# Attention matmuls in one float32r pass from pair 22 on, weights' sums moved to other stages, right pools at multiples of 64 bytes

## The chip, the cores and the metric

One core of one Trainium2 chip. The metric is device time in microseconds (us) of one execution; the runs shown are the median of three. Everything below is float32 in and out; float32r is the type in which TensorE takes a float32 word in one pass.

## The reference

Chunked attention, then two feed-forward layers, over 4608 tokens of 512 features:

```
for each batch (8), head (8), chunk of 64 tokens (9 of them), d = 64:
    s = q k^T / 8 ; p = exp(s - max) / (sum + 1e-9) ; o = p v
x  = o as [4608, 512]
h  = x @ w_in [512, 2048] ; g = h if h > 0 else exp(min(h, 0)) - 1 ; y = g @ w_out [2048, 512]
out = (sigmoid(y @ w_gate) * (y @ w_val)) @ w_out2      # w_gate, w_val [512, 1536], w_out2 [1536, 512]
```

Weights arrive as float64 and are converted on the chip.

## The kernel before

**Precision.** A product of two float32 matrices is made of three passes over float32r halves (`PASSES`, line 33): each operand is split in a high and a low part (`split`, line 94), and high-high, low-high and high-low are added in PSUM. The attention alone uses plain float32 matmuls, which TensorE carries out in several passes of its own: each stands twice in the records.

**Phase A** runs nine blocks of 512 tokens, each with 16 slots (`slot(s)`, line 358; s = 16 * block + f). A slot makes 12 matmuls `h` (`layer_1`, line 322: 128x512 columns) and 12 matmuls `y` for the slot two before (`layer_2`, line 330). Between them the two other engines make the activation: ScalarE (ACT) takes exp and relu (lines 302 and 305) and the high half (line 90), VectorE (DVE) the sum (line 308) and the low half (line 96).

**Attention is woven into the slots**, a pair of chunk groups (128x256 scores) in two slots, for the block after the current one. Even slot: `scores` (line 234, four matmuls of 64 columns; operands in `raw`, zero-padded on the host so that two chunks share one array), `softmax_max`, `softmax_exp`, `softmax_sum` (lines 248 to 264). Odd slot: `transposes` on TensorE (line 266), copied out by ACT (line 276), and in the next odd slot `values` (line 278) and `values_out`. 64 pairs go this way; 8 more open the program in `first_block`.

**Conversion of weights.** `convert` makes the first layer's weights in block 0. `convert_pairs` (line 566) makes the sums that the gate, value and output weights need (seven products of blocks in place of eight), 18 pairs of weight tiles. Each is a list of small steps in `todo`; `bg(n)` (line 102) takes n of them at four places of a slot. They spread over blocks 1 to 7, about three steps a slot, and their results go to DRAM (`wd`).

**Phase B.** Gate and value (`unit`, line 757): 36 units of 7 products, each product 12 matmuls of 384 columns; `xc`, the split input, is the moving operand and the weight tile the stationary one (line 772). Weight tiles are loaded ahead by `hold` (line 700), up to `RING` = 26 of 32 buffers. The output layer (`product`, line 897): 9 groups of 7 products, each 36 matmuls of 256 columns; here `gc`, the split gated input, is stationary (line 909).

**Where those operands lie.** `xc`, `gc`, `sg`, `vt` come from `get` (line 675), which takes the first name of `idle`: six buffers of pool `six_r`, on the right side of the memory, and seven of `six_l`, on the left. In the built program every `six_r` buffer begins 32 bytes past a multiple of 64, every `six_l` buffer and every weight tile at a multiple of 64. Followed through `idle`, the `xc` tiles of the six thirds of gate and value lie on the right in 6, 3, 4, 4, 3 and 4 of 7 cases (24 of 42; each tile serves six units), and 27 of 63 products' worth of `gc` tiles do.

Of the kernel before, what the change touches and what calls it, by code (L numbers as in the profile page):

```python
# [36 lines left out]
NP = NG // 2 - PB  # L37

# [4 lines left out]
FIRST_STEPS, A0_STEPS, A8_STEPS = 3, 9, 2  # L43
# [8 lines left out]
def kernel(  # L52
# [3 lines left out]
    qkv_1: bass.AP,  # L56
    w_in: bass.AP,
# [28 lines left out]
    ps_a = ctx.enter_context(tc.tile_pool(name="ps_a", bufs=2, space=bass.MemoryType.PSUM))  # L86
# [115 lines left out]
    def phase_a():  # L202
        with (
# [5 lines left out]
            e4 = c_p.tile([128, 4, CH + 1], F32, name="e4")  # L209

            raws, vals, st = {}, {}, {}

            def bank(n):
                return ps_a.tile([128, 512], F32, tag="a", name="bank")[:, 0:n]

            def load_raw(P):
                if P < NP:
                    raws[P] = a_p.tile([128, 2, 384], F32, tag="raw", name="raw")  # L220
                    nc.sync.dma_start(out=raws[P], in_=qkv_1[P][:, :, 0:384])

            def load_values(P):
                if 0 <= P < NP:
# [8 lines left out]

            def scores(P):
                ps, r = bank(256), raws.pop(P)
                st[P, "s"] = ps
                for i in range(2):
                    for a in range(2):
                        nc.tensor.matmul(  # L239
                            out=ps[:, (2 * i + a) * CH:(2 * i + a + 1) * CH],  # L240
                            lhsT=r[:, i, a * 128:(a + 1) * 128],
                            rhs=r[:, i, 256 + a * CH:256 + (a + 1) * CH],
# [3 lines left out]
                load_raw(P + 1)  # L246

            def softmax_max(P):
                s = st[P, "sc"] = a_p.tile([128, 4, CH], F32, tag="s", name="s")
                m = a_p.tile([128, 4, 1], F32, tag="m", name="m")  # L250
                ps = st.pop((P, "s"))
                ps = ps.rearrange("p (n k) -> p n k", n=4)
                nc.vector.tensor_reduce(out=m[:, :, 0], in_=ps, op=ALU.max, axis=AX.X)
                nc.vector.tensor_tensor(out=s, in0=ps, in1=m.to_broadcast([128, 4, CH]), op=ALU.subtract)
# [4 lines left out]
            def softmax_sum(P):  # L259
                d = a_p.tile([128, 4, 1], F32, tag="d", name="d")  # L260
# [16 lines left out]

            def values(P):
                t = st.pop((P, "t"))
                ps, r = bank(256), vals.pop(P)  # L280
                st[P, "v"] = ps
                for i in range(2):
                    for u in range(2):
                        nc.tensor.matmul(  # L284
                            out=ps[:, 128 * i + u * CH:128 * i + (u + 1) * CH],
                            lhsT=r[:, i, u * 128:(u + 1) * 128],
                            rhs=t[:, 128 * i + u * CH:128 * i + (u + 1) * CH],
# [70 lines left out]
            def slot(s, steps=0):  # L358
# [8 lines left out]
                def is_pair(n):  # L367
                    return 0 <= n < NP

# [721 lines left out]
```

## Time and profile before

| | |
|---|---|
| median of 3 runs | 1769.94 us (1769.7 to 1770.62) |
| the profiled execution | 1771.81 us, span 1770.0 us |
| PE (matmul) busy | 1750.8 us, 99% of the span |
| DVE, ACT busy | 1085.0 us (61%), 717.7 us (41%) |
| DMA | 289.5 MB, mean 164 GB/s |
| block 0 with what opens it | until about 140 us |
| blocks 1 to 8 | about 140 to 958 us |
| gate and value | 958 to 1496 us |
| output layer | 1496 to 1765 us |

How to read it: a matmul's record is longer than the array's work for it, since matmuls overlap; so TensorE's pace is read from one start to the next. Idle time of an engine is listed with what ended it.

### The profile page before, as it was taken

How to read it: one execution, taken by the hardware profiler on the slowest of the kernel's cores; microseconds unless marked ns; L12 is line 12 of the kernel's file. 1: busy time of each engine (PE TensorE's matmuls, PEld its weight loads, DVE VectorE, ACT ScalarE, POOL GpSimd, SP SyncE). 2: the span in 40 equal slices, each digit the busy share in tenths (PEclk: the TensorE clock that was granted, in tenths of full speed). 3: DMA queues.
4: the chain of work that ended last, by engine and by line, in shares of the span. 5: the costliest groups of instructions: out<-in, count | busy, mean ns of one | idle time of the engine just before them, and what ended most of it. 6: DMA issues, size and time to landing. Idle time of an engine off the chain costs nothing.

```text
span 1770.0 us, 25620 instructions
## 1 busy us (share of the span) xinstructions
PE 1750.8 (99%) x10012; PEld 1600.3 (90%) x10012; DVE 1085.0 (61%) x1811; ACT 717.7 (41%) x1254; POOL 143.6 (8%) x264
## 2 busy tenths in 40 slices
PE   7999999999999999999999999999999999999998
PEld 6888888888888888888888999999999999999998
DVE  7997565655645455465342565656565656777775
ACT  7775454544545454454443121212121212433433
POOL 1000000000100000000021111111111120000000
PEclk9899999999999999999999999999999999999999
DMA  6654454544534324343278748483848397645451
GB/s 231 199 183 128 146 155 134 155 153 128 178 116 143 114 89 131 116 143 104 68 235 228 231 118 275 119 274 118 275 117 275 119 327 217 177 138 150 136 150 48
DMA packets 183431, 289.50 MB, mean 164 GB/s; under 512 B 10000, under 2 KB 125712, under 8 KB 183312
## 3 DMA queue, kind: packets, MB, share of 16 engines
q1 hardware_dynamic: 137232, 147.87, 27.2%
q0 software_dynamic: 46080, 140.00, 25.8%
q8 instruction: 79, 1.29, 0.3%
q14 instruction: 40, 0.33, 0.1%
HBM read 207.62 MB, written 80.22 MB: 163 GB/s over the span
## 4 chain that ended last, share of the span: by engine, by line
PE 97%; ACT 1%; DMA 1%; DVE 0%; SPq 0%; issue 0%; ACTq 0%
PE h L189 23%; PE y L338 22%; PE bx L772 9%; PE by L772 8%; PE bz L772 8%; PE by L909 4%; PE bx L909 4%; PE bz L909 4%; PE bw L772 4%; PE bank L239 3%; PE bank L284 3%; PE bw L909 2%; PE bank L270 1%; DMA qkv<-in_qkv 0%; DMA ymid<-y 0%; ACT xr L521 0%
## 5 line engine op out<-in xcount | busy, mean ns | idle before, releaser
L189 PE MATMUL h<-xs,w 128*128 128x512 f32 x1728 | 435.4, 400 | 1.3 <-DVE xs L531 1.3
L338 PE MATMUL y<-g,w 128*128 128x512 f32 x1728 | 422.3, 393 | 0.0
L338 PEld LDWEIGHTS y<-g,w 128*128 128x128 f32 x1728 | 320.4, 188 | 66.0
L189 PEld LDWEIGHTS h<-xs,w 128*128 128x128 f32 x1728 | 317.3, 190 | 63.8 <-DVE xs L531 1.7
L308 DVE SCALAR_TENSOR_TENSOR elu<-h,elu 128x512 f32<-128x512 f32 x144 | 99.4, 690 | 172.3 <-ACT elu L305 172.1
L772 PE MATMUL bx<-xc,w 128*128 128x384 f32 x864 | 164.9, 339 | 1.9 <-ACT sg L794 1.9
L772 PE MATMUL by<-xc,w 128*128 128x384 f32 x864 | 163.8, 338 | 0.0
L772 PE MATMUL bz<-xc,w 128*128 128x384 f32 x864 | 163.5, 337 | 0.0
L302 ACT ACTIVATE elu<-h 128x512 f32<-128x512 f32 x144 | 85.8, 596 | 179.0 <-PE h L189 178.3
L772 PEld LDWEIGHTS bx<-xc,w 128*128 128x128 f32 x864 | 153.7, 189 | 2.3 <-ACT sg L794 2.2
L772 PEld LDWEIGHTS by<-xc,w 128*128 128x128 f32 x864 | 153.0, 188 | 0.0
L772 PEld LDWEIGHTS bz<-xc,w 128*128 128x128 f32 x864 | 152.7, 188 | 0.0
L96 DVE TENSOR_TENSOR g<-elu,g 128x512 fp32r<-128x512 f32 x128 | 88.1, 688 | 76.9 <-ACT g L90 76.6
L90 ACT CAST g<-elu 128x512 fp32r<-128x512 f32 x144 | 89.3, 620 | 83.5 <-PE y L338 55.3
L715 POOL DMA_DIRECT2D w<-wd_glu x147 | 77.7, 529 | 510.1 <-DVE xc L96 215.5
L807 ACT ACTIVATE sg<-bx 128x384 f32<-128x384 f32 x36 | 17.7, 491 | 221.6 <-PE bx L772 221.5
L815 ACT ACTIVATE sg<-sg 128x1152 f32<-128x1152 f32 x36 | 42.0, 1168 | 151.0 <-DVE sg L791 151.0
L305 ACT ACTIVATE elu<-elu 128x512 f32<-128x512 f32 x144 | 91.2, 633 | 1.9
L96 DVE TENSOR_TENSOR gc<-c,gc 128x768 fp32r<-128x768 f32 x72 | 65.6, 953 | 28.7 <-ACT gc L90 28.7
L772 PE MATMUL bw<-xc,w 128*128 128x384 f32 x432 | 81.6, 337 | 0.0
L909 PE MATMUL by<-w,gc 128*128 128x256 f32 x648 | 80.1, 282 | 0.0
L909 PE MATMUL bx<-w,gc 128*128 128x256 f32 x648 | 79.8, 281 | 0.0
(116 smaller groups left out, 2229.6 us busy)
## 6 DMA issues: line engine op xcount, KB each, us to landing
w<-wd_glu POOLq DMA_DIRECT2D x147, 512.0 KB, 5.1
gv<-sg SPq DMA_DIRECT2D x36, 768.0 KB, 6.1
c<-gv SPq DMA_DIRECT2D x72, 384.0 KB, 5.2
raw<-in_qkv SPq DMA_DIRECT2D x64, 384.0 KB, 3.5
vals<-in_qkv SPq DMA_DIRECT2D x64, 256.0 KB, 3.4
wd_glu<-h POOLq DMA_DIRECT2D x12, 1024.0 KB, 6.5
w<-wd_out POOLq DMA_DIRECT2D x21, 512.0 KB, 5.1
wd_glu<-h POOLq DMA_DIRECT2D x12, 768.0 KB, 4.2
```

The costliest lines, as they stand in the source:

```text
L90: nc.scalar.copy(out=out, in_=raw)
L96: lo_eng.tensor_sub(out=lo, in0=raw, in1=hi)
L189: nc.tensor.matmul(out=ps, lhsT=w[:, zw, kk * 128:(kk + 1) * 128], rhs=xs[key, kk][:, zx], start=(kk == 0 and n == 0), stop=(kk == KC - 1 ...
L239: nc.tensor.matmul(out=ps[:, (2 * i + a) * CH:(2 * i + a + 1) * CH], lhsT=r[:, i, a * 128:(a + 1) * 128], rhs=r[:, i, 256 + a * CH:256 + ( ...
L284: nc.tensor.matmul(out=ps[:, 128 * i + u * CH:128 * i + (u + 1) * CH], lhsT=r[:, i, u * 128:(u + 1) * 128], rhs=t[:, 128 * i + u * CH:128 ...
L302: nc.scalar.activation(out=e_t[s], in_=h_t[s], func=ACTF.Exp)
L305: nc.scalar.activation(out=e_t[s], in_=e_t[s], func=ACTF.Relu, scale=-1.0, bias=1.0)
L308: nc.vector.scalar_tensor_tensor(out=e_t[s], in0=h_t.pop(s), scalar=0.0, in1=e_t[s], op0=ALU.max, op1=ALU.subtract,)
L338: nc.tensor.matmul(out=y_t[j, e], lhsT=w[:, zw, e * 128:(e + 1) * 128], rhs=g[:, zx], start=(f == 0 and n == 0), stop=(f == F1 - 1 and n = ...
L715: nc.gpsimd.dma_start(out=t, in_=wd[m][q][:, (LEFT if m == "glu" else RIGHT)[i]])
L772: nc.tensor.matmul(out=ps[m, c], lhsT=w[:, b, zw, 128 * k:128 * k + 128], rhs=xc[j, i][:, zx, k], start=(i < 4 and k == 0 and p == 0), sto ...
L909: nc.tensor.matmul(out=po[c][:, m], lhsT=t[:, zx, q % 3, 128 * m:128 * m + 128], rhs=w[:, q % 2, zw], start=(i < 4 and q == 0 and p == 0 a ...
```

## The change

**Attention from pair 22 on** (`P32`; slots from `TURN` = 40, block 2, to the end of block 7: 42 pairs). Loads bring the values once, unpadded (`raw2`). `split_k` and `split_qkv` make float32r halves on the chip; q's high half stands in one half of the partitions and its low half in the other, so that one matmul of 256 columns against k's high and low parts gives a product of two halves: four matmuls of 256 columns for the scores, four for the values. The two column groups are added outside TensorE (`first_parts` on ACT, an add on DVE). The transposes on TensorE are gone: `blocks_out` transposes 32x32 blocks on DVE and moves them over partitions by eight DMAs of 16 KB on SP's queue; `transposes_split` makes the halves two slots later. The scores and the values share one pair of PSUM banks. TensorE, a pair's two slots, before (`bank`: attention's PSUM; `h`, `y`: the layer's):

```order
L284 MATMUL bank<-t,vals 128x64 x4
L189 MATMUL h<-xs_4115,w 128x512 x3
L189 MATMUL h<-xs_4118,w 128x512 x3
L189 MATMUL h<-xs_4121,w 128x512 x3
L189 MATMUL h<-xs_4124,w 128x512 x3
L270 MATMUL bank<-ident,p 128x128 x2
L338 MATMUL y_4315<-g,w 128x512 x3
L338 MATMUL y_4316<-g,w 128x512 x3
L338 MATMUL y_4317<-g,w 128x512 x3
L338 MATMUL y_4318<-g,w 128x512 x3
L239 MATMUL bank<-raw 128x64 x4
```

and now:

```order
L284 MATMUL banks<-kz,qv 128x256 x4
L194 MATMUL h<-xs_7378,w 128x512 x3
L194 MATMUL h<-xs_7381,w 128x512 x3
L194 MATMUL h<-xs_7384,w 128x512 x3
L194 MATMUL h<-xs_7387,w 128x512 x3
L445 MATMUL y_7596<-g,w 128x512 x3
L445 MATMUL y_7597<-g,w 128x512 x3
L445 MATMUL y_7598<-g,w 128x512 x3
L445 MATMUL y_7599<-g,w 128x512 x3
L383 MATMUL banks<-pt,qv 128x256 x4
```

The transposes' row has gone, and both attention rows have four matmuls of 256 columns in place of 64. DVE in two slots past slot 40, before:

```order
L253 TENSOR_REDUCE m<-bank 128x4
L254 TENSOR_TENSOR s<-bank,m 128x256
L601 TENSOR_SCALAR t<-t 128x512
L604 SCALAR_TENSOR_TENSOR t<-wraw,t 128x512
L96 TENSOR_TENSOR g<-elu,g 128x512
L261 TENSOR_REDUCE d<-e_111 128x4
L262 RECIPROCAL d<-d 128x4
L264 TENSOR_TENSOR p<-e_111,d 128x256
L308 SCALAR_TENSOR_TENSOR elu<-h,elu 128x512
L610 ISA t<-wraw,t 128x1024
L648 TENSOR_TENSOR h_6105<-s,h_6105 128x4x256
L96 TENSOR_TENSOR g<-elu,g 128x512
```

Now the even slot and the beginning of the odd one (`kz`, `qv`: halves of k, and of q and v; `pt`: halves of the transposed weights; `tt`, `dt`: the transposed blocks after and before the DMAs):

```order
L314 TENSOR_TENSOR s<-banks,s_5095 64x256 x2
L315 TENSOR_REDUCE m<-s 128x4
L316 TENSOR_TENSOR s<-s,m 128x256
L97 CAST pt<-tt 64x512
L101 TENSOR_TENSOR pt<-tt,pt 64x512
L323 TENSOR_REDUCE d<-e_112 128x4
L324 RECIPROCAL d<-d 128x4
L326 TENSOR_TENSOR p<-e_112,d 128x256
L343 STREAM_TRANSPOSE dt<-p 128x4x2x32
L101 TENSOR_TENSOR g<-elu,g 128x512
L415 SCALAR_TENSOR_TENSOR elu<-h,elu 128x512
L252 CAST kz<-raw 128x2x256
```

and the rest of the odd slot, up to the sum of the next slot:

```order
L252 CAST kz<-raw 128x2x256
L399 TENSOR_TENSOR xr_5049<-banks,s_5162 64x256 x2
L260 TENSOR_TENSOR kz<-raw,kz 128x2x256
L261 TENSOR_TENSOR qv<-raw,qv 64x2x256
L262 TENSOR_TENSOR qv<-raw,qv 64x2x256
L101 TENSOR_TENSOR g<-elu,g 128x512
L415 SCALAR_TENSOR_TENSOR elu<-h,elu 128x512
```

The weight conversion's rows (`t`, `h_6105`) have gone from these slots, and 13 instructions of the attention stand where 5 stood; the two last `qv` rows are what the next slot's scores wait for, the `pt` rows what the next slot's values wait for.

**Weights' sums.** Pairs 0 to 8 (`PAIRS_A`) are made in slots 16 to 39, six steps a slot; pairs 9 to 17 from slot 4 of block 8 on, four steps a slot from slot 5 on, and then one step after each product of gate and value, in buffers of the weight pool. Until all are made, `hold` keeps 19 tiles, not 26. DVE in a unit of gate and value, before:

```order
L829 TENSOR_TENSOR sg<-vt,sg 128x1152
L791 TENSOR_TENSOR sg<-bw,sg 128x384
L791 TENSOR_TENSOR vt<-bw,vt 128x384
L791 TENSOR_TENSOR sg<-by,sg 128x384
L791 TENSOR_TENSOR vt<-by,vt 128x384
L791 TENSOR_TENSOR sg<-bz,sg 128x384
L791 TENSOR_TENSOR vt<-bz,vt 128x384
```

and now (`ct`, `cs`, `ch`: a weight pair, its sums, their halves):

```order
L987 TENSOR_TENSOR sg<-vt,sg 128x1152
L745 SCALAR_TENSOR_TENSOR ct<-craw,ct 128x512
L948 TENSOR_TENSOR sg<-bw,sg 128x384
L948 TENSOR_TENSOR vt<-bw,vt 128x384
L751 ISA ct<-craw,ct 128x1024
L948 TENSOR_TENSOR sg<-by,sg 128x384
L948 TENSOR_TENSOR vt<-by,vt 128x384
L764 TENSOR_TENSOR cs<-ct 128x256
L765 TENSOR_TENSOR cs<-ct 128x256
L948 TENSOR_TENSOR sg<-bz,sg 128x384
```

Each product's two adds are followed by one step of the conversion.

**Right pools.** A pool of 32 bytes is opened first on the right side, and small tiles grow to multiples of 64 bytes. In the built program every `six_r` buffer now begins at a multiple of 64, and so do the new attention tiles.

```diff
+TURN = 40
+P32 = TURN // 2 + 2
+PAIRS_A = 9
...
+    pad_p = ctx.enter_context(tc.tile_pool(name="pad", bufs=1, side="right"))
+    pad_p.tile([128, 8], F32, name="pad")
...
+            def split_k(P):
+                k = kz[P] = s_p[0].tile([128, 2, 2, 256], F32R, tag="kz", name="kz")
+                nc.vector.tensor_copy(out=k[:, :, 0], in_=raws[P][:, :, 256:512])
+            def split_qkv(P):
...
+                nc.scalar.copy(out=t[h0, :, 0], in_=r[h0, :, 0:256])
+                nc.scalar.copy(out=t[h1, :, 1], in_=r[h1, :, 0:256])
+                nc.vector.tensor_sub(out=k[:, :, 1], in0=r[:, :, 256:512], in1=k[:, :, 0])
+                nc.vector.tensor_sub(out=t[h1, :, 0], in0=r[h0, :, 0:256], in1=t[h0, :, 0])
+                nc.vector.tensor_sub(out=t[h0, :, 1], in0=r[h1, :, 0:256], in1=t[h1, :, 1])
...
+                ps, k = banks[0], kz.pop(P)
                 for i in range(2):
+                    for u in range(2):
                         nc.tensor.matmul(
+                            out=ps[:, i, 256 * u:256 * u + 256].rearrange("p (z x) -> p z x", z=2),
+                            lhsT=qv[P][:, i, u, 0:128],
+                            rhs=k[:, i, :, u * 128:(u + 1) * 128],
...
+            def first_parts(P, what):
+                t = st[P, what + "1"] = s_p[0].tile([128, 4, CH], F32, tag="s1", name="s1")
+                for a, p in enumerate(halves):
+                    nc.scalar.copy(out=t[p], in_=parts_of(st[P, what], p, a)[0])
...
+                s1 = st.pop((P, "s1"))
+                for a, p in enumerate(halves):
+                    nc.vector.tensor_tensor(out=s[p], in0=parts_of(ps, p, a)[1], in1=s1[p], op=ALU.add)
...
+            def blocks_out(P):
...
+                for b in range(2):
+                    for w in range(4):
+                        nc.sync.dma_start(
+                            out=t[32 * b:32 * b + 32, w],
+                            in_=d[32 * w:32 * w + 32, b].rearrange("p n q -> p (n q)"),
...
+                            lhsT=qv[P][:, i, u, 128:256],
+                            rhs=t[:, 2 * i + u],
...
+            if most is None:
+                most = 32 - 6 - (0 if len(ready) == len(pairs) else 7)
             for k in uses[at:]:
+                if not made(k):
+                    break
...
+                bg(1)
...
         for f in range(F1):
-            slot((NB - 1) * F1 + f, A8_STEPS)
-            drain(f, slot)
-        bg(len(todo))
+            slot((NB - 1) * F1 + f, 4 if f > 4 else 0)
+            drain(f)
```

## Rows read from the trace of the kernel before

**Rows 1.** The page, busy time of the engines over the span.
```profile
PE 1750.8 (99%) x10012; PEld 1600.3 (90%) x10012; DVE 1085.0 (61%) x1811; ACT 717.7 (41%) x1254; POOL 143.6 (8%) x264
```

**Rows 2.** Timeline of PE, two slots past slot 40 (start us, us, line op out<-in xcount).
```profile
567.39 3.02 PE L338 MATMUL y<-g,w 128*128 128x512 f32 x12
570.24 1.00 PE L239 MATMUL bank<-raw 128*128 128x64 f32 x8
...
580.26 0.38 PE L270 MATMUL bank<-ident,p 128*128 128x128 f32 x2
580.40 3.02 PE L338 MATMUL y<-g,w 128*128 128x512 f32 x12
```

**Rows 3.** Timeline of PE in block 8, where no attention is left.
```profile
917.16 2.88 PE L189 MATMUL h<-xs,w 128*128 128x512 f32 x12
...
947.08 2.88 PE L338 MATMUL y<-g,w 128*128 128x512 f32 x12
```

**Rows 4.** Timeline of PE, three products of the output layer.
```profile
1722.30 4.39 PE L909 MATMUL bx<-w,gc 128*128 128x256 f32 x36
1726.52 4.48 PE L909 MATMUL by<-w,gc 128*128 128x256 f32 x36
1730.84 4.39 PE L909 MATMUL bz<-w,gc 128*128 128x256 f32 x36
```

**Rows 5.** Timeline of PE, four products of gate and value at the first turn.
```profile
1049.08 2.28 PE L772 MATMUL by<-xc,w 128*128 128x384 f32 x12
1051.20 2.27 PE L772 MATMUL bz<-xc,w 128*128 128x384 f32 x12
1053.31 2.24 PE L772 MATMUL bx<-xc,w 128*128 128x384 f32 x12
1055.39 2.24 PE L772 MATMUL bw<-xc,w 128*128 128x384 f32 x12
```

**Rows 6.** Timeline of PE, first product of unit 1 and first of the output layer.
```profile
979.18 2.28 PE L772 MATMUL bx<-xc,w 128*128 128x384 f32 x12
...
1495.71 4.39 PE L909 MATMUL bx<-w,gc 128*128 128x256 f32 x36
```

**Rows 7.** DVE and ACT groups by shape (out<-in xcount | busy us, mean ns of one | idle before).
```profile
L308 DVE SCALAR_TENSOR_TENSOR elu<-h,elu 128x512 f32<-128x512 f32 x144 | 99.4, 690 | 172.3 <-ACT elu L305 172.1
...
L254 DVE TENSOR_TENSOR s<-bank,m 128x256 f32<-128x256 f32 x64 | 27.2, 424 | 2.2
...
L598 DVE TENSOR_SCALAR t<-t 128x512 f32<-128x512 f32 x36 | 15.1, 418 | 10.8 <-ACT t L586 10.8
...
L262 DVE RECIPROCAL d<-d 128x4 f32<-128x4 f32 x64 | 11.4, 178 | 2.2
...
L90 ACT CAST g<-elu 128x512 fp32r<-128x512 f32 x144 | 89.3, 620 | 83.5 <-PE y L338 55.3 <-DVE elu L308 27.7 <-PE bank L239 0.2
...
L276 ACT COPY t<-bank 128x256 f32<-128x256 f32 x64 | 23.5, 367 | 0.0
```

**Rows 8.** Windows: us; busy us of PE, PEld, DVE, ACT, POOL; clock; DMA share, GB/s.
```profile
44.25:150.00 105.75, 105.09 (x515) 87.92 (x515) 103.54 (x214) 80.26 (x157) 0.71 (x1) 0.95 0.54 171
150.00:310.00 160.00, 160.00 (x812) 134.86 (x811) 94.88 (x186) 78.83 (x149) 12.30 (x19) 1.00 0.49 148
1135.00:1494.00 359.00, 359.00 (x2047) 359.00 (x2046) 213.79 (x333) 82.06 (x123) 52.34 (x99) 1.00 0.71 220
```

**Rows 9.** DMA issues and landing (KB each, median us), and SP's timeline.
```profile
four<-ymid SPq DMA_DIRECT2D x12, 128.0 KB, 4.6
...
961.59 2.49 SPq L356 DMA_DIRECT2D ymid<-y  x4
```

**Rows 10.** Timeline of PE and ACT where gate and value begin.
```profile
967.08 2.28 PE L772 MATMUL bz<-xc,w 128*128 128x384 f32 x12
...
970.68 0.48 ACT L794 COPY sg<-bx 128x384 f32<-128x384 f32 x1 [7.01 <-DMA ymid<-y]
...
977.09 2.25 PE L772 MATMUL bz<-xc,w 128*128 128x384 f32 x12
```

More of the change, by code (lines that the diff above doesn't have):

```diff
@@ new lines, in scores @@
+            def scores(P):
+                if P < P32:
+                    ps, r = bank(256), raws.pop(P)
+                    st[P, "s"] = ps
+                    for i in range(2):
+                        for a in range(2):
+                            nc.tensor.matmul(
+                                out=ps[:, (2 * i + a) * CH:(2 * i + a + 1) * CH],
+                                lhsT=r[:, i, a * 128:(a + 1) * 128],
+                                rhs=r[:, i, 256 + a * CH:256 + (a + 1) * CH],
+                                start=True,
+                                stop=True,
+                            )
+                    if P + 1 < P32:
+                        load_raw(P + 1)
+                    return
+                ps, k = banks[0], kz.pop(P)
@@ L379, in slot @@
                     softmax_max(P)
+                if even and is_pair(P, P32):
+                    softmax_exp(P)
+                if even and is_pair(P - 1, P32):
+                    transposes_split(P - 1)
+                if even and is_pair(P, P32):
+                    softmax_sum(P)
+                    blocks_out(P)
+                if not even:
+                    if is_pair(N, P32):
+                        split_k(N)
+                    if is_pair(V, P32):
+                        values_out(V)
+                    if is_pair(N, P32):
+                        split_qkv(N)
                 bg(q[0])
@@ L396, in slot @@
                     elu_split(s - 1)
-                if even and is_pair(P):
+                if even and 0 <= P < P32:
                     softmax_exp(P)
-                now = not even and is_pair(T) and s >= F1
+                now = not even and 0 <= T < P32 and s >= F1
                 if now:
@@ L404, in slot @@
                     transposes_out(T)
-                if even and PB <= P < NP:
+                if even and PB <= P < P32:
                     softmax_sum(P)
@@ L609, in add, with quarters @@
         def add(p, i):
-            nc.vector.tensor_add(out=half(p, i), in0=half(p, i), in1=raws.pop(2 * p + i)[:, :, 0])
-            load(2 * p + i + 1)
+            nc.vector.tensor_add(out=half(p, i), in0=half(p, i), in1=raws.pop((p, i))[:, :, 0])
+            load(tiles.index((p, i)) + 2)
+        def quarters(p, k):
+            return now[p, k].bitcast(F32).rearrange("p (n k) -> p n k", n=4)
         def sums(p):
-            t, _ = parts(p)
-            s = now[p, "s"] = pool.tile([128, 4, 256], F32, tag="s", name="s")
+            now[p, "s"] = alloc("s", F32)
+            t, s = quarters(p, "t"), quarters(p, "s")
             if pairs[p][3]:
@@ L623, in sums_of_sums @@
         def sums_of_sums(p):
-            t, s = parts(p)[0], now[p, "s"]
+            t, s = quarters(p, "t"), quarters(p, "s")
             if pairs[p][3]:
@@ L654, in convert_pairs @@
         load(0)
-        for p in range(len(pairs)):
+        load(1)
+        for p in which:
             for i in range(2):
```

272 lines of the change are left out of this document (180 added, 92 removed).

## The prediction

> **What bounds the kernel now.** I read the busy times first: PE has a matmul under way for 1750.8 of 1770.0 us, no other engine is above 61% [rows 1]. So time is won only where TensorE's own work shrinks, and lost where it is made to wait. The records overlap, so I take TensorE's pace from one start to the next in its timeline. Two slots with attention last 580.40 - 567.39 = 13.01 us [rows 2]. In block 8, without attention, twelve matmuls of 512 columns take (947.08 - 917.16) / 11 = 2.72 us [rows 3], and two slots hold four such dozens: 10.88 us. The attention of one pair thus costs TensorE 2.13 us: eight records for the scores, as many for the values, two transposes.
>
> **What it would cost now.** Eight float32r matmuls of 256 columns with a weight load each: that is what the output layer is made of, 36 in 4.22 or 4.32 us, 117 or 120 ns each [rows 4]. The 4.32 belongs to a product whose stationary tiles lie at multiples of 64 bytes, as all the new tiles do, so I take 120 ns: 0.96 us a pair, a gain of 1.17 us, for 42 pairs **49.1 us**. Below, 117 ns gives 50.0. Above: the values' right operand is read in runs of 32 elements, which no row shows; if that halved the pace, such a matmul would cost what one of 512 columns does, 2.72 / 12 = 0.227 us, and four of them 0.43 us a pair more: 18 us of the gain lost. I take the contiguous price, since two of three operands are read as in rows 4, and keep 18 us for the range. The transposes' work goes to DVE and SP's queue, below.
>
> **The right pools.** In gate and value a product is 12 matmuls whose moving operand is an `xc` tile on one side or the other. Around the first turn [rows 5] the product at 1049.08 (right) takes 2.12 us, the next (left, after a right one) 2.11, the two after it (left after left) 2.08. The right buffers begin 32 bytes past a multiple of 64, the left ones at a multiple. From unit 1 to the output layer 245 products take 1495.71 - 979.18 = 516.53 us, 2.108 each [rows 6]; at 2.08 all of them save 245 x 0.028 = **6.9 us**. In the output layer it is the other way: the operand is stationary, and 4.22 belongs to two right tiles, 4.32 to two left ones [rows 4]. Moved to multiples of 64, 27 of 63 products' worth of tiles lose 0.10 us each: **2.7 us**. Net gain 4.2 us; bounds are 0 (it is not the address) and 6.9 (only the moving operand counts).
>
> The Trainium skill speaks against this part ("SBUF — State Buffer", Specifications (TRN2)): lines are 16 bytes long, and a start 32 bytes off begins one just as well. By that rule the sum would be 4.2 us higher. The two paces of rows 5 don't follow from it, unless the side itself makes them.
>
> **DVE, which takes over the work.** By like rows [rows 7] a pair's two slots cost it: eight instructions of 512 columns with two tensors (two sums, two low halves of the layer; low halves of k, of q and v in two, of the transposed weights) at 0.69 = 5.52; nine of 256 (two adds, maximum, subtraction, sum, product, block transpose, two adds of the values) at 0.42 = 3.82; two casts of 512 at 0.42, as the single-tensor instruction of L598, = 0.84; the reciprocal 0.18. With 64 partitions I count the columns alone. A block's four low halves of x and two copies of y add 6 x 0.69 / 8 = 0.52. Sum 10.88 us in 11.84, 92%; with casts and transpose at 0.69, 11.69, 99%. Does that starve TensorE? In block 0 DVE was busy 103.54 of 105.75 us, 98%, and PE 105.09 [rows 8]: a nearly full DVE hides there, since the layer's results are due a slot later.
>
> What is due sooner, counted from the even slot's start. Scores end at 0.48, ACT's two copies (0.37) at 1.2, DVE's four steps of 0.42 at 2.9, cast and low half of the previous pair's transposed weights at 4.0 (they cover the exponent), sum to block transpose at 5.5. The values start at 5.92 and need ACT's second copy of 0.62, about 4.6: 1.3 us to spare. In the odd slot DVE gets the relu at about 6.5 and ends the sum at 7.2, the cast at 7.6, the values' adds at 8.5, three low halves at 10.5; the next scores start at 11.84: again 1.3 us. The eight DMAs: SP issues four in 2.49 us, 0.62 each, so 5.0, and the smallest transfer shown, 128 KB, lands in 4.6 [rows 9]: 9.6 us from 5.5 on, due at 11.84 + 2.9 for DVE, 9.2 later, and 10.5 later before TensorE feels it. So I cost DVE, ACT and the queue at **nothing**, with margins of about 1 us. Behind them on SP stand the next load, which waits for the q and v halves and is due a slot later, and once a block four stores of y, 2.49 us, which the same margin takes. At slot 40 the first cast of k waits for the last conversion results to leave the buffers that it reuses; they were issued a slot before, so I count that at nothing too.
>
> **The moved conversion.** In blocks 1 and 2 DVE was busy 94.88 of 160 us, 59% [rows 8]; three steps more in a slot of 6.5 us at up to 0.69 make it 91%, under block 0's 98%: nothing. Block 8: two sums and halves 1.38, four steps of about 0.57 on average, one or two preparations of x of about 1 us: 5.2 of 5.44; nothing. In gate and value DVE was busy 213.79 of 359 us, 60% [rows 8], 8.8 of a unit's 14.8; seven steps make 12.8. POOL's queue carries raw loads and results among the weight tiles that are held 19 products ahead, 40 us (26 before, so a few more tiles are loaded twice): nothing.
>
> One hand-over has no cover. Where gate and value begin, three products take 977.09 - 967.08 = 10.01 us in place of 3 x 2.12: 3.65 lost, while ACT waits for the last stores of y [rows 10]. These now share the DMA engines with the conversion. Bounds: nothing left of the loss, or twice it. I take half as much again, **1.8 us**.
>
> **Sum.** 1771.81 - 49.1 - 6.9 + 2.7 + 1.8 = 1720.3 us against the profiled execution's own time, which was 1.87 above the median; as a median **1718 us**. With the bounds of the parts that stay likely: 1712 (50.0 gained, no loss at the hand-over) to 1736 (values at half pace).
>
> **Rivals.**
> *DVE becomes the bound, and the kernel slower.* All depends on DVE's in-order queue doing other work while ACT makes what it waits for: two pairs of copies (1.48), the exponent (about 0.37), casts of q and v (1.24) and of g (1.24), 4.33 us a pair [rows 7]. With none of it covered a pair takes 10.88 + 4.33 = 15.21 us, 3.37 more than TensorE's 11.84: 142 us, 1860 in all. It decides against the change from 1.24 us over 11.84 on, that is, if over 2.2 of the 4.33 stand bare. For it: 92%, and each half is needed soon. Against it: block 0, and the order, which puts the previous pair's halves beside the exponent. 5%. If only a part shows, or the casts cost 0.69, TensorE loses 0.2 to 1 us a pair: 1726 to 1760, 9%.
> *The block transposes come late.* Eight transfers of 16 KB, smaller than any shown. If they land 1 us past the margin, every pair waits: 42 us, 1760. Against: the 9.6 us above already take the landing of 128 KB in a busy stage. 6%. The Trainium skill ("DMA: Bandwidth & Descriptors", Rules for kernel authors) would have small transfers coalesced, because under 64 KB one pays mostly overhead; no row has such a transfer.
> *The pools change nothing* (the side, not the address, sets the pace): 1722. 10%; for it only that sides and addresses coincide in every row.
> *Gate and value wait.* In units 5 and 11 the next third's splits (seven at about 1 us) and seven steps stand together: 7.5 + 4.0 + 7.2 = 18.7 us of DVE in 14.6. Its results are due two products later, 4.2 us, just what is missing. If not covered: 8 us, 1726. 7%.
>
> **How the numbers follow.** The forecast itself 63%. The range takes in the pools' rival, gate and value's, the half pace of the values and small parts of the first: 1711 to 1740. A difference under 0.2%, 3.5 us, can't be told from none here. Faster: everything but the heavy DVE case and the end of its light one, 93%; the same 2%, slower 5%.
>
> **What would show it.** Right: two slots of 11.84 us from slot 42 on, with attention rows of about 0.48 from start to start; DVE busy about 92% of blocks 3 to 7; products of gate and value at 2.08 on either side, of the output layer all at 4.32. Wrong: idle time of PE before `banks` with DVE or ACT as releaser (first rival), DVE idle before `pt` with a DMA as releaser (second), products still at 2.12 on the right (third), PE idle before `bx` or `by` in units 5 and 11 (fourth).

## The result and the profile after

The changed kernel takes 1727.39 us (median of 4 runs, 1726.71 to 1727.93) against 1770.09 for the kernel before: a ratio of 0.9758, 95% interval 0.9741 to 0.9775. It is faster, as forecast, and 9 us above the forecast of 1718. The profiled execution took 1727.2 us, its span 1725.3.

TensorE is still the bound (the page, busy time over the span, as [rows 1]):

```profile
PE 1697.6 (98%) x9592; PEld 1548.7 (90%) x9592; DVE 1307.6 (76%) x2309; ACT 860.8 (50%) x1542; POOL 173.1 (10%) x314
```

A pair of the attention, as [rows 2] (timeline of PE, start us, us; `L284` are the scores, `L383` the values):

```profile
377.44 0.64 PE L284 MATMUL banks<-kz,qv 128*128 128x256 f32 x4
377.92 2.91 PE L194 MATMUL h<-xs,w 128*128 128x512 f32 x12
380.67 2.88 PE L445 MATMUL y<-g,w 128*128 128x512 f32 x12
383.38 0.65 PE L383 MATMUL banks<-pt,qv 128*128 128x256 f32 x4
383.87 2.91 PE L194 MATMUL h<-xs,w 128*128 128x512 f32 x12
386.62 2.88 PE L445 MATMUL y<-g,w 128*128 128x512 f32 x12
389.34 0.64 PE L284 MATMUL banks<-kz,qv 128*128 128x256 f32 x4
```

From scores to scores 389.34 - 377.44 = 11.90 us, against 13.01 before and 11.84 forecast. The attention's rows take 0.48 and 0.49 from start to start, as forecast; the dozens of 512 columns stand at 2.71 to 2.75. A pair gives back 1.11 us.

Stretches as in [rows 8] (us; busy us of PE, PEld, DVE, ACT, POOL; clock; DMA share, GB/s), blocks 1 and 2, then 3 to 7:

```profile
150.00:310.00 160.00, 154.55 (x784) 129.50 (x783) 123.11 (x258) 90.56 (x184) 33.56 (x52) 1.00 0.70 216
320.00:810.00 490.00, 488.66 (x2297) 407.62 (x2295) 421.15 (x844) 339.18 (x642) 0.00 (x0) 1.00 0.22 65
```

In the first TensorE lacks 5.45 us of 160, where nothing was lacking before: that is new. In the second DVE is busy 86%, not 92%, and TensorE lacks 1.34 us. (A pair's attention is sixteen instructions of DVE, not 13. DVE's records, added one by one, make 439.3 us here, 90%; they overlap by 18.4 us, and the forecast added them.)

Gate and value at the first turn, as [rows 5], and two products of the output layer, as [rows 4], with the start of the next (that row is cut off by the window):

```profile
1030.16 2.24 PE L929 MATMUL by<-xc,w 128*128 128x384 f32 x12
1032.24 2.27 PE L929 MATMUL bz<-xc,w 128*128 128x384 f32 x12
1034.34 2.24 PE L929 MATMUL bx<-xc,w 128*128 128x384 f32 x12
1036.42 2.24 PE L929 MATMUL by<-xc,w 128*128 128x384 f32 x12
```

```profile
1681.79 4.48 PE L1067 MATMUL by<-w,gc 128*128 128x256 f32 x36
1686.11 4.41 PE L1067 MATMUL bz<-w,gc 128*128 128x256 f32 x36
1690.35 3.85 PE L1067 MATMUL bx<-w,gc 128*128 128x256 f32 x31
```

The product at 1030.16 and that at 1036.42 have right tiles: 2.08 us, 2.12 before. A left one after a right one (1032.24) still takes 2.10. Followed through `idle`, the output layer's product at 1681.79 has two left tiles and takes 4.32 us, as before; the one at 1686.11 has two right tiles and takes 4.24, where such a product took 4.22 before and 4.32 was forecast.

Summed from one matmul's start to the next, in the two profiled executions: gate and value 535.0 to 525.3, output layer 269.3 to 271.1, the two layers with the attention and all their waits 936.2 to 898.0, the opening 21.0 to 22.5. That makes 44.6 of the spans' 44.7 us. Of the 1.9 us that the output layer lost, 1.1 are two short waits in its second product (0.66 and 0.42 us over a matmul's usual start to start); the kernel before had none there (third line):

```profile
1454.06 0.74 PE L1067 MATMUL bw<-w,gc 128*128 128x256 f32 x4 [0.49 <-ACT gc L95]
1455.05 4.10 PE L1067 MATMUL bw<-w,gc 128*128 128x256 f32 x32 [0.25 <-DVE gc L101]
1499.93 4.48 PE L909 MATMUL bw<-w,gc 128*128 128x256 f32 x36
```

The new wait in blocks 1 and 2 has two places, 163.4 and 270.2. At the first, TensorE and ACT:

```profile
160.71 3.01 PE L194 MATMUL h<-xs,w 128*128 128x512 f32 x12
166.22 0.41 PE L332 MATMUL bank<-ident,p 128*128 128x128 f32 x2 [2.50 <-DVE p L326]
```

```profile
163.13 0.62 ACT L787 CAST ch<-cs 128x512 fp32r<-128x512 f32 x1 [7.84 <-DMA wd_glu<-ch]
163.65 0.61 ACT L95 CAST g<-elu 128x512 fp32r<-128x512 f32 x1
164.17 0.41 ACT L319 ACTIVATE e<-s 128x256 f32<-128x256 f32 x1
```

The transposes come at 166.22, 5.5 us after a dozen that lasts 2.86. They wait for DVE's `p`, this for ACT's exponent at 164.17, and that stands in ACT's order behind the rounding of a weight pair's last quarter (`L787`), which waited 7.84 us for the landing of a store. The rounding writes to one of three buffers, and the buffer's last content was still on its way to DRAM. No engine was full: one waited in order.

### The profile page after: what moved, and what is told of

Same layout as the page of the kernel before. It is cut to its first block, busy times and chain, and to the rows that moved or that the text cites. A ratio compares the mean times of both kernels' runs of the same rounds, so it can differ in the third digit from the quotient of the medians.

```text
span 1725.3 us, 26183 instructions
## 1 busy us (share of the span) xinstructions
PE 1697.6 (98%) x9592; PEld 1548.7 (90%) x9592; DVE 1307.6 (76%) x2309; ACT 860.8 (50%) x1542; POOL 173.1 (10%) x314
## 4 chain that ended last, share of the span: by engine, by line
PE 78%; DVE 11%; ACT 5%; DMA 3%; issue 3%; SPq 0%; POOL 0%; DVEq 0%; ACTq 0%; POOLq 0%
PE y L445 15%; PE h L194 15%; PE bx L929 8%; PE by L929 8%; PE bz L929 8%; PE by L1067 4%; PE bz L1067 4%; PE bw L929 4%; PE bx L1067 4%; PE bw L1067 2%; DMA wd_glu<-ch 1%; PE banks L383 1%; PE banks L284 1%; DVE elu L415 1%; DVE t L145 1%
## 5 line engine op out<-in xcount | busy, mean ns | idle before, releaser
L194 PE MATMUL h<-xs,w 128*128 128x512 f32 x1728 | 427.2, 395 | 1.3 <-DVE xs L660 1.3
L445 PE MATMUL y<-g,w 128*128 128x512 f32 x1728 | 416.5, 390 | 0.0
L872 POOL DMA_DIRECT2D w<-wd_glu x161 | 86.3, 541 | 271.0 <-DVE xc L101 123.8
L101 DVE TENSOR_TENSOR g<-elu,g 128x512 fp32r<-128x512 f32 x128 | 86.6, 677 | 12.6 <-ACT g L95 11.0
L301 ACT COPY s<-banks 64x256 f32<-64x256 f32 x168 | 60.9, 362 | 55.9 <-PE banks L284 52.7
L95 ACT CAST gc<-s 128x768 fp32r<-128x768 f32 x54 | 42.4, 833 | 77.2 <-DVE s L1023 43.4
```

Of the source, the lines that this page charges most:

```text
L95: nc.scalar.copy(out=out, in_=raw)
L101: lo_eng.tensor_sub(out=lo, in0=raw, in1=hi)
L194: nc.tensor.matmul(out=ps, lhsT=w[:, zw, kk * 128:(kk + 1) * 128], rhs=xs[key, kk][:, zx], start=(kk == 0 and n == 0), stop=(kk == KC - 1 ...
L301: nc.scalar.copy(out=t[p], in_=parts_of(st[P, what], p, a)[0])
L445: nc.tensor.matmul(out=y_t[j, e], lhsT=w[:, zw, e * 128:(e + 1) * 128], rhs=g[:, zx], start=(f == 0 and n == 0), stop=(f == F1 - 1 and n = ...
L872: nc.gpsimd.dma_start(out=t, in_=wd[m][q][:, (LEFT if m == "glu" else RIGHT)[i]])
```

## The experiments

All times stand beside 1769.3 to 1770.8 us of the kernel before, run with them. "Gate and value" and "output layer" are sums from start to start, as above: 525.25 and 271.1 in the changed kernel.

### The order of the conversion

```diff
+                        late=True,
...
                 queue((add, p, i))
+                if late and i == 0 and p > which[0]:
+                    queue((high, p - 1, 5))
+                    queue((rest, p - 1, 5))
...
+            if late and p < which[-1]:
+                queue((rest, p, 3))
+                continue
             queue((rest, p, 3), (high, p, 5))
             queue((rest, p, 5))
```

> The changed kernel (1727.4 us) with one thing moved: in blocks 1 and 2 the rounding and the rest of the last quarter of each weight pair come eight steps later, after the sign step of the next pair. Theory: TensorE's two stalls there (2.66 us at 163.4 and 2.40 us at 270.2) come from ScalarE, which waits in order for a buffer of three whose store to DRAM has not landed (idle 7.84 and 8.41 us); by the time of the moved step the store of the buffer's last content has landed, so both stalls go and the time falls by about 5 us, to 1722.3. Rival: VectorE has too much to do there (78% busy), whatever the order; then the stalls stay, 2 us or more each, and the time stays within 1 us of 1727.4.

In the edit the two steps come six steps later, behind the `add` of the next pair's first tile (not eight, behind the sign step). 1719.31 us, ratio 0.9712 (0.9699 to 0.9725). The same place, TensorE's timeline, and the window of blocks 1 and 2:

```profile
160.19 3.02 PE L194 MATMUL h<-xs,w 128*128 128x512 f32 x12
163.05 0.38 PE L332 MATMUL bank<-ident,p 128*128 128x128 f32 x2
```

```profile
150.00:310.00 160.00, 160.00 (x812) 134.66 (x811) 127.63 (x260) 95.45 (x190) 32.48 (x51) 1.00 0.72 222
```

The transposes follow after 2.86 us, TensorE lacks nothing in 160 us, and DVE is busier than before (127.63 against 123.11). ACT's waits for these stores, from 140 to 310 us, fall from 43.9 us (nine waits, up to 8.4) to 3.9. So it was ACT's place in the order and not DVE's load: the rival falls. Of the 8.1 us, 5.1 are the two waits; the two waits of 0.9 and 1.1 us at the turn (301.6 and 315.7) are gone as well, but they came and went in other runs that leave that place alone, so I don't credit them to the edit.

### The first slot of a block

```diff
+                if even and f == 0 and is_pair(P - 1, P32):
+                    transposes_split(P - 1)
                 if even and is_pair(P):
                     softmax_max(P)
...
-                if even and is_pair(P - 1, P32):
+                if even and f > 0 and is_pair(P - 1, P32):
                     transposes_split(P - 1)
```

> The changed kernel (1727.4 us) with one thing moved: in the first slot of blocks 3 to 7 the split of the transposed weights' sums stands ahead of the softmax's maximum instead of behind it. Theory: the values' products at each block's start wait 0.36 to 0.72 us for ScalarE's copies of that split, because VectorE's four low halves of the new block's input stand ahead of it; 1.7 us of VectorE's work (the sum, the maximum, the subtraction) taken from its path remove the five waits, 2.2 us in all, to 1725.2. Rival: the split is late for another reason (the eight transfers that bring the blocks together); then the split starts no earlier, the waits stay, and the time stays within 0.7 us of 1727.4.

1725.85 us, 0.9749 (0.9736 to 0.9763): not to be told from the changed kernel by time alone. TensorE at the start of block 4 in the changed kernel, then here (the third line is the scores that follow), with DVE's order here:

```profile
452.02 2.88 PE L445 MATMUL y<-g,w 128*128 128x512 f32 x12
455.45 0.75 PE L383 MATMUL banks<-pt,qv 128*128 128x256 f32 x4 [0.55 <-ACT pt L361]
```

```profile
451.50 2.88 PE L445 MATMUL y<-g,w 128*128 128x512 f32 x12
454.22 0.65 PE L383 MATMUL banks<-pt,qv 128*128 128x256 f32 x4
460.18 0.98 PE L284 MATMUL banks<-kz,qv 128*128 128x256 f32 x4
```

```profile
450.43 0.69 DVE L415 SCALAR_TENSOR_TENSOR elu<-h,elu 128x512 f32<-128x512 f32 x1
451.04 0.41 DVE L97 CAST pt<-tt 64x512 fp32r<-64x512 f32 x1
```

3.43 us from the dozen to the values there, 2.72 here; the split starts right behind the sum, 0.46 us before the dozen at 451.50, while in the changed kernel it starts at 453.61, 1.59 us after the dozen at 452.02; the eight transfers land before 449.3 in both. All five waits are gone, and the rival (late transfers) falls. But most of the gain comes back one slot later: at each of the five block starts the scores behind take 0.82 us (461.00 - 460.18, where the next row starts) in place of 0.48, and the profile names DVE's last `qv` instruction as what they wait for. Of 2.1 us removed, 1.7 return.

### More work for DVE

```diff
-                    split(e_t.pop(s), g[:, 0], g[:, 1], nc.scalar, nc.vector)
+                    e = e_t.pop(s)
+                    split(e, g[:, 0], g[:, 1], nc.scalar, nc.vector)
+                    if 3 * F1 <= s < 8 * F1:
+                        nc.vector.tensor_sub(out=g[:, 1], in0=e, in1=g[:, 0])
```

> The changed kernel (1727.4 us) with one subtraction of VectorE done twice in every slot of blocks 3 to 7 (the rest of the first layer's activations, 0.65 us, written again with the same values): 1.3 us more a pair, 86% busy becomes 97%. Theory: VectorE does not bound these blocks below 100%, but its slack is what takes up the block starts; so the waits at the five block starts grow from 0.4 to 0.7 us to some 2 us each and few others come: 5 to 10 us more, 1732 to 1738. Rival, VectorE bound by its order already: a third or more of the added work shows, 80 slots by 0.65 us being 52 us, so 1745 or more. Rival, slack everywhere: within 1 us of 1727.4.

1734.09 us, 0.9801 (0.9787 to 0.9814), 6.7 us more. The window of blocks 3 to 7, then TensorE's wait for the values' operand there (us in total, times, longest), here and in the changed kernel:

```profile
320.00:810.00 490.00, 481.65 (x2258) 400.53 (x2257) 463.55 (x906) 333.53 (x631) 0.00 (x0) 1.00 0.22 65
```

```profile
PE banks L383 <- ACT pt L361: 8.4, 10, 1.1
```

```profile
PE banks L383 <- ACT pt L361: 1.3, 5, 0.5
```

DVE is at 463.55 of 490, 95%. Of 52 us of added work under 7 show, nearly all in ten waits in the first pairs of each block. DVE does not bound these blocks, but its slack is what takes up a block's start.

### The attention taken out again

```diff
-TURN = 40
+TURN = 124
...
-        "qkv": pairs(third.reshape(-1, H // 2, 128, 512))[P32:],
+        "qkv": pairs(third.reshape(-1, H // 2, 128, 512))[P32 - 1:],
```

(The second line only keeps an array from being empty; no pair reads it.)

> The changed kernel (1727.4 us) without its float32r attention: no pair is turned over, and the conversion of nine weight pairs is spread over slots 16 to 123; the rest is as changed. Theory: the 42 pairs give 47.8 us in TensorE's own time, and 9.2 us of TensorE's waits came with them (5.1 at the conversion in blocks 1 and 2, 1.9 at the turn, 2.2 at the starts of blocks 3 to 7); without both 1766, of which 6 of gate and value and 3.7 of the hand-over stay gained against before. Rival: part of what was gained is not the attention's, so that the time falls to less than 1760; or the hand-over's stall of 3.65 us at the start of gate and value comes back, 1770.

1763.46 us, 0.9966 (0.9952 to 0.9979), 2.5 us under the theory and above the first rival's 1760, so the attention is worth 36.1 us, net of the waits that the denser conversion brings (it is spread thinner here). Gate and value stay at 525.25, with no stall at their start; the two layers and the attention take 935.9, as before the change (936.2), and 37.9 more than in the changed kernel. The output layer takes 269.9: the two waits in its second product are not there.

### The pools

Each of these runs moves the large tiles (gate and value's moving operand, the output layer's stationary one) and nothing else of the changed kernel.

```diff
+        pad2_p = ctx.enter_context(tc.tile_pool(name="pad2", bufs=1, side="right"))
+        pad2_p.tile([128, 8], F32, name="pad2")
         six = {"r": ctx.enter_context(tc.tile_pool(name="six_r", bufs=6, side="right", reuse_waits="tile"))}
```

> The changed kernel (1727.4 us) with the six large right tiles of the gate, value and output layers moved by 32 bytes, as they lay before the change; the attention is untouched. Theory: TensorE's products with a moving operand of 384 columns take 176.9 ns from tiles at 32 bytes past a multiple of 64, and 173.6 ns on it, so gate and value get 6.1 us longer, and the output layer 1.9 us shorter again (its stationary operand behaves the other way round, 117.2 against 120 ns): 1731.6. Rival: the side counts, or what else shares the memory, not the address: then every product of gate and value stays at 2.08 us and the time stays within 0.7 us of 1727.4.

1724.85 us, 0.9747 (0.9734 to 0.9761); gate and value 524.78, output layer 271.24. My theory falls: 32 bytes off a multiple of 64, and nothing is lost. (These tiles begin 160 bytes past a multiple of 256, which the table below takes up.)

```diff
-            t = six[p].tile([128, 1536], dtype, tag="six", name=key)
+            t = six[p].tile([128, 1552], dtype, tag="six", name=key)
+            t = t[:, 8:1544] if key == "gc" else t[:, 0:1536]
```

> The changed kernel (1727.4 us) with the tiles that hold the output layer's stationary operand begun 32 bytes into their buffers, on both sides, while gate and value's stay on multiples of 64. Theory: the matmuls of 256 columns there take about 119.6 ns with tiles on multiples of 64 and 117.2 ns at 32 bytes past one; of 2268 of them that makes 5.3 us: 1722. Rival: the difference of the output layer belongs to the side or to which tiles the other operand lies in; then the output layer stays at 271.1 us and the time within 0.7 us of 1727.4.

1726.95 us, 0.9753 (0.9739 to 0.9766): the output layer falls by 2.2 us to 268.9, not by 5.3, and gate and value rise by 1.9 to 527.18, though their tiles stand on multiples of 64. Neither theory said that. 0.7 of the 2.2 us is the first of the two waits, absent here. And the longer buffers also moved gate and value's tiles, to 0, 64, 128 and 192 bytes past a multiple of 256.

```diff
+        pad2_p = ctx.enter_context(tc.tile_pool(name="pad2", bufs=1, side="right"))
+        pad2_p.tile([128, 24], F32, name="pad2")
```

> The changed kernel (1727.4 us) with the six large right tiles 96 bytes lower, so that they begin 96 bytes past a multiple of 128, exactly as in the kernel before (the run with them at 32 past one kept all products at 2.08 us). Theory: it is this address, 32 bytes ahead of a multiple of 128, that makes a product from a right tile 2.12 us, so gate and value get about 5 us longer (1728 matmuls by 3 ns), and the output layer 1 us shorter: 1731. Rival: the address has no part in it, and the longer products of before came from what ran beside them; then the products stay at 2.08 us and the time within 2 us of 1727.4.

1727.54 us, 0.9765 (0.9751 to 0.9778); gate and value 526.32, 1.1 longer, not 5. What 128 bytes could not tell apart, 256 could: this run's tiles lie 96 bytes past a multiple of 256, those of the kernel before 224. So the next run put them at exactly the old address.

```diff
-    pad_p = ctx.enter_context(tc.tile_pool(name="pad", bufs=1, side="right"))
+    pad = ExitStack()
+    pad_p = pad.enter_context(tc.tile_pool(name="pad", bufs=1, side="right"))
...
+        pad.close()
         six = {"r": ctx.enter_context(tc.tile_pool(name="six_r", bufs=6, side="right", reuse_waits="tile"))}
```

> The changed kernel (1727.4 us) with the six large right tiles at exactly the address of the kernel before (the 32 bytes ahead of them are given back when the gate and value layers begin); the attention is untouched. The runs so far, sorted by the moving operand's first byte past a multiple of 256, give 173.2 ns at 192, 173.3 at 160, 173.6 at 96, 173.9 at 128, 174.5 at 64, 176.0 at 0, and in the kernel before alone 176.6 at 224. Theory: the address in 256 bytes decides; then 1728 products take 176.6 ns again, gate and value get 5.8 us longer, the output layer stays, 1733. Rival: what the kernel before does beside those products made them longer; then they stay near 173.3 ns and the time within 2 us of 1727.4.

1731.32 us, 0.9780 (0.9767 to 0.9794); gate and value 531.35: 6.1 us more; output layer 270.27, 0.9 less, of which 0.25 are shorter waits in its second product. TensorE's products there, then those of the run at 96 bytes (right, right, left in both):

```profile
1036.81 2.28 PE L931 MATMUL by<-xc,w 128*128 128x384 f32 x12
1038.93 2.28 PE L931 MATMUL bz<-xc,w 128*128 128x384 f32 x12
1041.05 2.27 PE L931 MATMUL bx<-xc,w 128*128 128x384 f32 x12
```

```profile
1036.86 2.25 PE L931 MATMUL by<-xc,w 128*128 128x384 f32 x12
1038.95 2.24 PE L931 MATMUL bz<-xc,w 128*128 128x384 f32 x12
1041.03 2.27 PE L931 MATMUL bx<-xc,w 128*128 128x384 f32 x12
```

From start to start 2.12 and 2.12 against 2.09 and 2.08: the old pace is back with the old address, beside the new kernel's work. The rival falls. Eleven profiled executions (before, changed, the late quarter, and all runs that move these tiles, those below too), a matmul's mean from start to start, by the first byte of the operand's tile past a multiple of 256 (the outer 5% on either side left out):

| bytes past a multiple of 256 | 0 | 32 | 64 | 96 | 128 | 160 | 192 | 224 |
|---|---|---|---|---|---|---|---|---|
| gate and value, moving, 384 columns, ns | 176.0 | - | 174.5 | 173.3 | 173.9 | 173.3 | 173.2 | 176.6 |
| output layer, stationary, ns | - | 119.8 | - | 116.7 | 119.9 | 118.2 | 117.8 | 117.6 |

The columns 0, 32 and 64 stand on the one or two runs with longer buffers. And a mean hides that the tile read just before counts too: with left tiles at 128, a left product takes 2.08 us behind another left one, but 2.11 behind a right one at 224, 192 or 96, and 2.09 behind one at 160; with all tiles at 96 (below) every product takes 2.08.

### Together

First the two orders (edits as above) with the output layer's tiles at 96 bytes past a multiple of 128, in longer buffers:

```diff
-            t = six[p].tile([128, 1536], dtype, tag="six", name=key)
+            t = six[p].tile([128, 1568], dtype, tag="six", name=key)
+            o = 0 if key != "gc" else 24 if p == "l" else 8
+            t = t[:, o:o + 1536]
```

> Three things at once on the changed kernel: the late last quarter (measured alone 1719.3), the earlier split of the weights' sums in a block's first slot (alone 1725.9), and the output layer's stationary tiles 96 bytes past a multiple of 128, with gate and value's at 0 and 64. In the run with these tiles 32 bytes into buffers of another size, matmuls at 96 took 117.6 ns and those at 32 118 to 120, against 120.4 on the left and 118.6 on the right in the changed kernel; 2268 of them at 117.6 make 4.5 us less. Theory: the three add up, 1719.3 - 1.5 - 4.5 = 1713. Rival: the edge's gain is taken by the next wait and the tiles' by gate and value's, which got 1.9 us longer in that run: 1718.

1718.51 us, 0.9713 (0.9699 to 0.9726): its rival. The output layer falls by 4.3 us (0.7 of it the first of its two waits), gate and value, now partly at 0 and 64 past 256, rise by 2.1. Then pads in place of the longer buffers, all tiles at 96 past 256:

```diff
+        pad2_p = ctx.enter_context(tc.tile_pool(name="pad2", bufs=1, side="right"))
+        pad2_p.tile([128, 24], F32, name="pad2")
...
+        pad3_p = ctx.enter_context(tc.tile_pool(name="pad3", bufs=1))
+        pad3_p.tile([128, 56], F32, name="pad3")
         six["l"] = ctx.enter_context(tc.tile_pool(name="six_l", bufs=7, reuse_waits="tile"))
```

> The late last quarter and the earlier split of the weights' sums (both as before), and all thirteen large tiles, left and right, 96 bytes past a multiple of 256. Theory: by the address in 256 bytes the moving operand takes 173.6 ns there (173.9 on the left and 173.2 on the right in the changed kernel: 0.35 us more in all), the stationary operand 116.8 ns (119.9 left, 117.8 right: 1296 by 3.1 and 972 by 1.0 make 5.0 us less); with 8.1 us of the late quarter and 1.5 us of the split that makes 1713 to 1715, since the two kept only part of their sum in the last run of all three. Rival: the side or the distance of the tiles from one another decides and not the address; then the output layer stays within 1.5 us of 271 and the time at 1718.

1715.84 us, 0.9691 (0.9677 to 0.9704), 0.8 over the upper end; the forecast took 1.5 us for the split, of which the scores behind take most back here too. Gate and value 524.17, output layer 265.71, 5.4 less: the address holds for both sides. Three products of the output layer, 4.20 each on the left as on the right:

```profile
1673.88 4.37 PE L1078 MATMUL bz<-w,gc 128*128 128x256 f32 x36
1678.09 4.36 PE L1078 MATMUL bx<-w,gc 128*128 128x256 f32 x36
1682.29 4.37 PE L1078 MATMUL bw<-w,gc 128*128 128x256 f32 x36
```

Then the turn two pairs earlier, `TURN = 36`, `PAIRS_A = 8`:

> The run with all tiles at 96 bytes, with the turn to float32r two pairs earlier (slot 36) and eight weight pairs converted ahead of it instead of nine. Theory: each pair is worth 1.14 us of TensorE, the conversion is 6.8 steps a slot instead of 6.4, and the ninth pair fits into the gate and value layers: 2.3 us less than that run, 1711 to 1713. Rival: the denser conversion or the pair that comes later makes TensorE wait (a stall in blocks 1 and 2, or of the weights in the gate and value layers): equal or longer.

1709.96 us, 0.9659 (0.9646 to 0.9673), the fastest; 1 us under the lower end. The spans differ by 3.4 us, of which 2.3 were due; 0.9 of the rest is the output layer, where the two waits of the second product are gone.

And four pairs earlier, `TURN = 32`, `PAIRS_A = 7`, five steps a slot in block 8:

> As the run before, two pairs earlier again (slot 32), seven weight pairs ahead of it at 7.4 steps a slot, and five steps a slot instead of four in block 8. Theory: 4.6 us less than the run with all tiles at 96 bytes, 1709 to 1711. Rival: VectorE in blocks 1 and 2 (some 85% busy then) lets the transposes come late again, by 0.5 us or more in most slots, which takes back the gain or more: 1713 to 1725.

1717.19 us, 0.9698 (0.9685 to 0.9712). A miss, and not by the rival I named: gate and value are at 532.63, because of one wait at their start (TensorE, ACT, and POOL's queue ahead of it):

```profile
919.56 2.24 PE L940 MATMUL bz<-xc,w 128*128 128x384 f32 x12
927.47 2.93 PE L940 MATMUL bx<-xc,w 128*128 128x384 f32 x8 [5.67 <-ACT sg L962]
```

```profile
926.93 0.48 ACT L962 COPY sg<-bx 128x384 f32<-128x384 f32 x1 [10.70 <-DMA ymid<-y]
```

```profile
914.79 0.53 POOL L721 DMA_DIRECT2D craw<-in_w_val  x1 [1.03 <-DMA craw<-in_w_val]
916.01 0.53 POOL L883 DMA_DIRECT2D w<-wd_glu  x1 [0.69 <-DMA w<-wd_glu]
```

ACT's first copy waits 10.70 us for the last stores of y, since it writes into memory that they still read, and the fifth product starts at 927.47, some 5.8 us late. Gate and value lost 8.5 us against the run at slot 36: behind the wait, fifteen matmuls start 0.32 us apart in place of 0.17, at a granted clock of half (1.2 GHz; windows as above, the clock is the third number from the end):

```profile
927.40:930.50 3.10, 3.03 (x9) 3.04 (x10) 3.06 (x6) 2.97 (x6) 0.00 (x0) 0.50 1.12 381
```

In the kernel before it was the same at this place: of its 3.65 us [rows 10], 2.0 are the wait and the rest ten matmuls 0.32 us apart, at a granted clock of 0.50 from 972.0 to 975.4. In the changed kernel ACT's wait was 2.82 us and hidden, and POOL's queue stood still for 12.13 us before it:

```profile
929.66 0.48 ACT L951 COPY sg<-bx 128x384 f32<-128x384 f32 x1 [2.82 <-DMA ymid<-y]
```

```profile
916.30 0.53 POOL L872 DMA_DIRECT2D w<-wd_glu  x1 [0.99 <-DVE cs L770]
928.97 0.71 POOL L792 DMA_DIRECT2D wd_glu<-ch  x1 [12.13 <-DVE ch L791]
```

POOL's next store waited there for DVE, and the loads behind it with it, while SP issued y's stores at 924.77: few loads ran beside them. The DMA share is 0.66 from 924.8 to 929.5, and each store lands within 2.6 to 2.8 us. In this run POOL goes on issuing loads, the DMA share is 1.10 from 914.2 to 926.9, and the stores take 6.8 to 10.2 us. The other traces agree: in all eleven with POOL held 11.8 to 12.6 us around y's stores the stores land within 2.1 to 3.0 us and there is no stall. In the kernel before, POOL issued loads beside the stores (960.54, 963.30, 965.42; it stood still for 11.60 us only after them), the share was 0.98, and the stores took 5.3 to 6.8. One thing more differs: SP's own loads of x go out from 917.38 here, beside the stores, and from 932.48, after them, in the changed kernel. Their part is not separated.

## Why the prediction was right and wrong

**Right:** sign, range and the main term. A pair costs 11.90 us in place of 11.84, so 42 of them give 46.6 us, not 49.1 (the `h` dozens beside them stand at 2.75 in place of 2.72); 120 ns a matmul was right (0.48 for four), and the values' right operand, read in runs of 32, costs the same. The transfers of 16 KB are no wait: the rival of the late blocks falls. DMA issues of the changed kernel, KB each, median us to landing:

```profile
tt<-dt SPq DMA_DIRECT2D x336, 16.0 KB, 1.8
```

The Trainium skill ("DMA: Bandwidth & Descriptors", Rules for kernel authors) speaks against transfers under 64 KB; here eight of 16 KB landed in 1.8 us each, under a DMA share of 0.22, and TensorE waited for none of them (DVE once, 0.8 us).

**"The moved conversion: nothing" failed**, by 5.1 us. I set DVE's busy time against block 0's 98% and left ACT out, whose order puts the weights' rounding ahead of the exponent, and left the store's landing out, for which the rounding waits. [rows 8] could not show it: in block 0 the halves are not stored.

**"1.3 us to spare" failed in one slot of sixteen**, 2.2 us in all. I spread a block's four low halves of x over its eight pairs (0.52 a pair); they stand together in one slot, 2.5 us, just ahead of the step with 1.3 us of margin. The other margin of 1.3 us, ahead of the scores, is as thin there: when the split goes first, the scores wait instead, and 1.7 of the 2.1 us come back. That DVE does not bound these blocks was right: at 95% the time rises by 6.7 us, not by the 52 added.

**At the turn**, 1.9 us in the profiled execution where I counted nothing; it is not in every run and stays open.

**The pools: gate and value's term was right in size, the output layer's was not, and the rule was wrong.** 6.9 forecast in gate and value, 6.1 shown by the undoing; a left product behind a right one kept its 2.11 us, which [rows 5] had shown and the sum overlooked. In the output layer 2.7 were to be lost because right tiles would take 4.32 us at a multiple of 64; they take 4.24. Of the 1.9 us measured, 1.1 are the two waits, and the address cost 0.6 (by the undoing) to 0.8. But "multiples of 64 bytes" is not what decides: 96 and 160 past 256, which are no such multiples, are as fast as 192, and 0, which is one, is as slow as the old 224. The rival "the side sets the pace" falls, and so does the sum by lines of 16 bytes (the Trainium skill, "SBUF — State Buffer", Specifications (TRN2)): all starts in the table are multiples of 16, and the paces differ by 3 ns in 173 and in 117. What the chip does with these 256 bytes is open; only the operand's address and pace are shown.

**The hand-over had the wrong sign.** I took 1.8 us more for DMA engines shared with the conversion; 3.65 were gained: the conversion also held POOL's queue back at that moment, and the stores landed sooner. The run at slot 32 shows the side that I had expected, a wait of 5.8 us and 8.5 lost in all. That POOL's hold is the cause is read from the fourteen traces, which agree; no run changed it alone, so it is not shown, and the hold itself was luck: nothing in the prediction looked for it.

**The sum.** Of 6.9 us between the profiled 1727.2 and the 1720.3 worked out: waits +10.3 (5.1, 1.9, 2.2, and 1.1 in the output layer), the pair's price +2.5, gate and value's address +0.8, opening +1.5 (it lies between 21.0 and 22.7 us in the fourteen traces, so much of this is scatter), hand-over -5.45, output layer's address -1.9, and -0.8 that I can't place. Two misses of over 5 us nearly cancelled, which was luck; the pair's price and gate and value's address were not. Gate and value's rival (units 5 and 11) falls: the only waits there were at their start.

## What to carry to other kernels

When work is moved beside other work, follow each in-order engine's queue through the moved steps and ask what each step waits for, a store's landing and a buffer's return above all; a share of busy time says nothing of it. A margin that is an average over a block is not there in the slot where the block's own work stands together. A wait that is removed can come back at the next step with as little margin, so add up the whole stage after an edit, not the place alone. And test an address effect by putting back the exact old address, before a rule is made of it.

## What was not expected of the hardware

Matmuls of 384 columns differ by 3.4 ns (173.2 to 176.6) and those of the output layer by 3.2 ns (116.7 to 119.9) with the operand's place in 256 bytes, and what is slow for the moving operand (224: 176.6) is fast for the stationary one (117.6). Placing all thirteen tiles at 96 took 5.4 us off the output layer and 1.1 off gate and value, at the price of 320 bytes a partition.

After some stops of TensorE its granted clock fell from 1.00 to half (1.2 GHz) for a while: after 2.0 us at the hand-over of the kernel before, after 5.8 us in the run at slot 32, and after 2.6 us at 269.75 in the run on a block's first slot (0.52 from 272.2 to 275.7). After 2.65 and 2.38 us in blocks 1 and 2 of the changed kernel it stayed at 1.00. These cases don't show what decides.
